# Gate logits with the turned tokens held still and eight gate columns moving, and counts one sub-step after them

## The chip, the cores and the metric

The kernel runs on one core of a Trainium2 chip. The metric is the device time of one execution in microseconds, the median of several runs. The profile is of one execution; its engines are called PE (matmuls; PEld are its weight loads), DVE, ACT, POOL and SP, and SP issues most of the transfers.

## What is computed

A causal long convolution of x (8 x 5696 x 128) with a filter h of the same length, by FFT, and on its output a mixture of eight experts in which each token goes to the one expert with the largest gate logit:

```
y = irfft(rfft(x, 2*S) * rfft(h, 2*S))[:, :S]        # x: (8, 5696, 128), h: (5696, 128)
y = y.reshape(45568, 128)
logits = y @ w_gate                                   # w_gate: (128, 8)
e = argmax(logits); p = softmax(logits)[e]            # one expert a token
out = p * (relu(y @ w1[e]) @ w2[e])                   # w1: (8, 128, 1024), w2: (8, 1024, 128)
```

## The kernel before

The batch is worked in three groups of 2, 3 and 3 sequences. Each group passes three stages: `phase_a` (one half of the forward transform, PSUM tiles `pa`), `phase_b` (the other half, product with the filter's spectrum, first half of the inverse) and `phase_c`, the last half of the inverse with the gating. Tokens are then scattered by POOL, row by row, into a DRAM table `SR` that is sorted by expert, and the experts work on tiles of 256 sorted rows.

`phase_c` goes over slots (16 in the first group, 24 in the second and third) of six blocks of 120 tokens, each slot in two sub-steps of three blocks. One sub-step (the loop over `n` and `k`) issues:
- `synth`: the inverse transform's matmuls into `yp`. `settle` copies them to `rt`, the rows that will be scattered, after the `yield`; the DVE addition at its start (line 739 of before) writes the row numbers once a slot.
- `turn`: three transposes (`flip`, line 182) of `rt` into the PSUM tile `tp`, one sub-step after `synth`. `turned` copies them to `yt`, 128 features by 120 tokens a block.
- `logit`: two sub-steps after `synth`, three matmuls that hold the gate's columns (padded to 32) and move a block of 120 tokens, each into its own 32 rows of the tail of `tp`. Each is two instructions on PE, since the data is plain float32. `logit_out` copies the 96 x 120 strip to `lt` on ACT.
- `score`, in the first sub-step of a slot only: into the PSUM tile `gb` go the counts of the slot before (one-hot `oh` times a matrix of ones and times a triangle), and the two strips of this slot, transposed so that tokens lie on partitions.
- a step or two of the next group's `phase_a` (`guest`), whose matmuls write `pa`.

After the `yield`, DVE runs `route` (`lmax`, `ls`, `w`, `wm`, the one-hot `oh`, the weight of the row) of one slot and `rank` (running counts `cum`, `base`, the row's place `rk`, `pi`) of the slot before it, their instructions alternating (`zipped`). `divide` splits the next input into two parts (`vr`, on ACT and DVE). `rank` puts six scatters on the list `sorts`; `sort_one` issues them on POOL, each tied to one of the PE or ACT instructions of its sub-step. When the last slot of a part of the tokens is ranked, `tables` works out which expert each tile of that part has, and the tile's gathers (`xr`, from `SR`) and weights (`wb`) may be issued on SP.

The experts are one stream, `pipeline`: an expert step is `mh` (line 1147, first layer, two 128-column pieces), ACT and DVE make `hs` of it, and two steps later `ma` (line 1168, second layer). Four steps make a tile; the input rows of a tile are turned in `mx`, printed as `mxNone` for the first. There are 182 tiles, 26 of them of the first part of the tokens; a tile is usable when its part is sorted, tabled and some virtual time old (`SETTLED`).

The order of all this on each engine is not written out. `run` holds a virtual time for each stream, takes the one that is earliest and adds what it yields: an expert step yields `STEP` (1420), a sub-step of `phase_c` yields `STEP` times `BESIDE` or `ENDING`, or less while it is `alone`. Engines then run in the order in which instructions were issued. PSUM tiles of `phase_c` rotate through four banks (`cx`) beside the experts.

## Time and profile before

| | us |
|---|---|
| median of 3 runs (lowest, highest) | 2227.01 (2226.05, 2228.76) |
| the profiled execution | 2223.97 |
| its span in the profile | 2222.2 |
| gating of the first group, alone | about 278 to 400 |
| scatters end, first expert tiles start | about 400 to 445 |
| second group's `phase_b`, then its gating | 445 to 716, 716 to 958 |
| its end, before the third group's `phase_b` | 958 to 1010 |
| third group's gating | 1353 to 1616 |
| expert tiles alone | from about 1680 to the end |

The mean granted TensorE clock was 0.976. Times within the profile count from the start of the span. The bounds of the stages are read from the lines that are active; experts run beside all that comes after about 430. In the rows, `L182` and the like are lines of the kernel before, `out<-in` names the tile written and those read, and an `x6` behind a row is a group of six instructions that follow each other. "Idle before" in brackets is how long the engine had nothing to run, and what ended that.

### The profile page before, as it was taken

What the parts mean: (1) busy time and instruction counts of PE and PEld (TensorE: products, weight loads), DVE (VectorE), ACT (ScalarE), POOL (GpSimd) and SP (SyncE); (2) the same over time, 40 slices, a digit from 0 to 9 for tenths busy, and PEclk for the clock granted to TensorE, in tenths of its full rate; (3) what the DMA queues carried; (4) which work ended last, traced back from release to release, by engine and by line L of the source; (5) the groups of instructions that cost most, each with busy time, mean ns of one, the idle gap of its engine ahead of it and who ended that gap; (6) DMA issues with size and microseconds to landing.
All of it is one profiled execution on the core that took longest, in us unless ns stands there. A gap on an engine that the chain in (4) does not pass through costs nothing. (4 is left out here: it accounts for less than half of the span.)

```text
span 2222.2 us, 47032 instructions
## 1 busy us (share of the span) xinstructions
PE 2078.4 (94%) x14198; PEld 1753.2 (79%) x14198; DVE 1556.4 (70%) x3731; ACT 1100.6 (50%) x2359; POOL 1285.2 (58%) x1486
## 2 busy tenths in 40 slices
PE   7899888599999999988999999999998999999997
PEld 5688655366667888876777779888888999999997
DVE  3588745599997788868988985777764555555554
ACT  4588644233334666643443445555544444444443
POOL 5366548776663388872565661787873444444442
PEclk9999999899999999999999999999999999999999
DMA  9889999699998888967898977777644543444430
GB/s 296 289 280 322 315 348 305 174 277 267 287 283 227 236 272 240 261 195 208 244 263 227 261 242 210 196 204 199 182 152 151 172 139 109 146 138 144 139 121 27
DMA packets 235225, 486.04 MB, mean 219 GB/s; under 512 B 33285, under 2 KB 147074, under 8 KB 234971
## 3 DMA queue, kind: packets, MB, share of 16 engines
q1 hardware_dynamic: 211035, 435.93, 65.4%
q0 software_dynamic: 23936, 47.09, 6.8%
q8 instruction: 115, 1.88, 0.4%
q14 instruction: 139, 1.14, 0.2%
HBM read 593.26 MB, written 173.52 MB: 345 GB/s over the span
## 5 line engine op out<-in xcount | busy, mean ns | idle before, releaser
L1155 DVE SCALAR_TENSOR_TENSOR hs<-mh,hs 128x512 fp32r<-128x512 f32 x728 | 500.8, 690 | 398.3 <-ACT hs L1153 326.9
L1147 PE MATMUL mh<-xtb,wb 128*128 128x256 f32 x4368 | 690.0, 294 | 33.9 <-DMA wb<-WD 18.7
L1153 ACT ACTIVATE hs<-mh 128x512 fp32r<-128x512 f32 x728 | 435.0, 598 | 495.3 <-PE mh L1147 379.5
L1147 PEld LDWEIGHTS mh<-xtb,wb 128*128 128x128 f32 x4368 | 585.6, 190 | 103.3 <-issue 44.8
L1168 PE MATMUL ma<-hs,wb 128*128 128x256 f32 x4368 | 655.8, 286 | 7.8 <-DMA wb<-WD 7.8
L1168 PEld LDWEIGHTS ma<-hs,wb 128*128 128x128 f32 x4368 | 568.3, 190 | 9.4 <-DMA wb<-WD 9.1
L644 POOL DMA_INDIRECT SR<-rt,pi x384 | 401.1, 1045 | 208.7 <-PE pa L305 52.3
L1223 POOL DMA_INDIRECT out<-xr x252 | 245.8, 975 | 311.2 <-DVE xr L1186 267.9
L544 POOL TENSOR_TENSOR zt<-zt,xs 128x384 f32<-128x384 f32 (+1 forms) x280 | 297.3, 1071 | 113.0 <-DVE xs L536 86.7
L568 ACT COPY vt<-vp 96x384 f32<-96x384 f32 (+1 forms) x300 | 148.9, 496 | 344.3 <-PE vp L553 314.6
L553 PE MATMUL vp<-zt,mi 128*96 128x384 f32 (+1 forms) x720 | 258.4, 454 | 8.7 <-DVE xs L536 5.3
L517 PE MATMUL xp<-uq,mt 96*128 96x384 f32 (+1 forms) x720 | 262.2, 460 | 3.1 <-ACT vt L568 1.1
L529 DVE TENSOR_TENSOR zt<-xp,hh 128x384 f32<-128x384 f32 (+1 forms) x300 | 174.0, 580 | 59.9 <-PE xp L517 54.7
L1223 POOL DMA_INDIRECT out<-xb x112 | 109.1, 974 | 169.0 <-ACT ot L1178 109.1
L553 PEld LDWEIGHTS vp<-zt,mi 128*96 128x96 f32 x720 | 112.4, 163 | 102.8 <-issue 53.5
L536 DVE SCALAR_TENSOR_TENSOR xs<-xp,hh 64x384 f32<-64x384 f32 (+1 forms) x300 | 175.7, 586 | 6.0
L305 PE MATMUL pa<-xc,fcr 120*120 120x512 f32 x576 | 165.6, 419 | 14.3 <-ACT xc L283 6.4
L534 DVE TENSOR_TENSOR xs<-xp,hh 64x384 f32<-64x384 f32 (+1 forms) x300 | 173.2, 577 | 6.0
L638 POOL TENSOR_TENSOR c_fcs<-c_fcs 120x64 f32<-120x64 f32 (+2 forms) x384 | 154.7, 403 | 11.4
L517 PEld LDWEIGHTS xp<-uq,mt 96*128 96x128 f32 x720 | 123.8, 195 | 33.9 <-issue 15.5
L305 PEld LDWEIGHTS pa<-xc,fcr 120*120 120x120 f32 x576 | 98.2, 186 | 49.6 <-ACT xc L283 7.2
L319 DVE COPY ut<-pa 120x512 f32<-120x512 f32 x96 | 65.9, 687 | 92.9 <-PE pa L305 81.6
(128 smaller groups left out, 2304.4 us busy)
## 6 DMA issues: line engine op xcount, KB each, us to landing
wb<-WD SPq DMA_DIRECT2D x728, 512.0 KB
vq<-V SPq DMA_DIRECT2D x64, 720.0 KB
U<-ut SPq DMA_DIRECT2D x48, 720.0 KB
uq<-U SPq DMA_DIRECT2D x60, 576.0 KB
V<-vt SPq DMA_DIRECT2D x60, 576.0 KB
xr<-SR SPq DMA_DIRECT2D x182, 130.0 KB
xt<-x SPq DMA_DIRECT2D x96, 240.0 KB
hh<-HS SPq DMA_DIRECT2D x120, 192.0 KB
```

Of the source, the lines that this page charges most:

```text
L305: done = nc.tensor.matmul(banks[m][:QN, :], lhs, rhs, start=(k == 0), stop=(k == len(ops) - 1))
L517: nc.tensor.matmul(xj, mt[:, k0 + j, :], uc.rearrange("p (b d) -> p b d", d=D), start=True, stop=True)
L529: nc.vector.tensor_tensor(out=zt, in0=x3, in1=hv[:, 0].broadcast_to([P] + wide), op=ALU.mult)
L536: nc.vector.scalar_tensor_tensor(out=xs[to], in0=x3[at], scalar=-1.0, in1=him, op0=ALU.mult, op1=ALU.mult)
L544: eng.tensor_tensor(out=zt, in0=zt, in1=xs, op=ALU.add)
L553: nc.tensor.matmul(vp[:K2, j * cw : (j + 1) * cw].rearrange("p (b d) -> p b d", d=D), mi[:, k0 + j, :], zt.rearrange("p b (j d) -> p b j d ...
L644: s = nc.gpsimd.indirect_dma_start(out=SR[:, :], out_offset=IndirectOffsetOnAxis(ap=pi[:, b : b + 1], axis=0), in_=rt[:, b, :], in_offset= ...
L1147: nc.tensor.matmul(hp[:, u, :], wb[:, a, f, :], xt[:, b, :], start=(n == 0), stop=(n == 2))
L1153: done = nc.scalar.activation(hs[:, 0], hp, AF.Relu)
L1155: nc.vector.scalar_tensor_tensor(out=hs[:, 1], in0=hp, scalar=0.0, in1=hs[:, 0].bitcast(F32), op0=ALU.max, op1=ALU.subtract)
L1168: nc.tensor.matmul(accs[t], wb[:, a, f, :], hs[:, b, u, :], start=(k == 0 and u == 0 and n == 0), stop=(k == NPAIR - 1 and u == 1 and n == 2),
L1223: sc = nc.gpsimd.indirect_dma_start(out=out[:, :], out_offset=IndirectOffsetOnAxis(ap=xr[:, s, D + 1 : D + 2].bitcast(I32), axis=0), in_=x ...
```

## The change

The logits are made by matmuls whose stationary operand is the turned block `yt` (128 x 120) and whose moving operand is the gate's eight columns, so that tokens come out on partitions and eight columns a block lie side by side. There are six for a slot, two instructions each, all in one sub-step, three after the `synth` of the slot's first half. `logit`, `logit_out`, the strips `lt` and their transposes are gone, and the tile `gb` holds logits only. The counts of a slot are made in the sub-step after its logits, in the tail of that sub-step's `tp`, behind the guest's `pa` (while the group is alone, in a bank of their own). `rank` follows in that sub-step together with `weigh` (the row's weight, formerly the end of `route`), and `route` stands alone in the other. The ranks of a slot thus come two sub-steps earlier than before, and the loop is two sub-steps shorter. The guest hands back all of its instructions as ties for scatters, the wait in `tables` is one `yield` shorter, and the small constants are 24 columns narrower.

```diff
...
-LOGIT = (2, 2, 2)
...
-    wg = part_of(32)
+    wg = part_of(E)
...
-            done = None
+            done = []
             for _ in range(min(count, self.M - self.m)):
-                done = self.step(self.m)
+                done.append(self.step(self.m))
                 self.open.append(self.m)
                 self.m += 1
             return done
...
-        lgs, cnts, lbank, lts = {}, {}, {}, {}
-
...
-        def score(n, m):
+        lgs, cnts, exps, ranks = {}, {}, {}, {}
+
+        def score(n):
             sp = bank(f"gb{g}_{n}", "mx")
-            if 0 <= m < nu:
-                oh2 = gates[m].rearrange("p b e -> p (b e)")
-                nc.tensor.matmul(sp[:, :w], ones, oh2, start=True, stop=True)
-                nc.tensor.matmul(sp[:MP, 128 : 128 + w], lt, oh2, start=True, stop=True)
-                cnts[m] = (
-                    sp[:, :w].rearrange("p (b e) -> p b e", e=E1),
-                    sp[:MP, 128 : 128 + w].rearrange("p (b e) -> p b e", e=E1),
-                )
-            if 0 <= n < nu:
-                lw = 32 * cb
-                for k in range(nsub):
-                    flip(sp[:MP, 256 + k * lw : 256 + (k + 1) * lw], lts.pop((n, k)), lw)
-                lgs[n] = sp[:MP, 256 : 256 + ns * 32].rearrange("p (b e) -> p b e", e=32)[:, :, :E]
+            lg = sp[:MP, : ns * E].rearrange("p (b e) -> p b e", e=E)
+            yt = yts.pop(n)
+            for b in range(ns):
+                nc.tensor.matmul(lg[:, b], yt[:, b, :], wg, start=True, stop=True)
+            lgs[n] = lg
+
+        def count(n, tp):
+            if state["alone"] or tp is None:
+                cb_, lo = bank(f"cb{g}_{n}", "mx"), 0
+            else:
+                cb_, lo = tp, 512 - 2 * w
+            oh2 = gates[n].rearrange("p b e -> p (b e)")
+            nc.tensor.matmul(cb_[:, lo : lo + w], ones, oh2, start=True, stop=True)
+            nc.tensor.matmul(cb_[:MP, lo + w : lo + 2 * w], lt, oh2, start=True, stop=True)
+            cnts[n] = (
+                cb_[:, lo : lo + w].rearrange("p (b e) -> p b e", e=E1),
+                cb_[:MP, lo + w : lo + 2 * w].rearrange("p (b e) -> p b e", e=E1),
+            )
 
         def route(n):
-            rt = rts[n]
...
             gates[n] = oh
-            yield
+
+        def weigh(n):
+            rt, ex = rts[n], exps.pop(n)
...
             with nc.allow_low_precision("whole numbers"):
                 nc.vector.tensor_reduce(out=pi, in_=rk, axis=AX.X, op=ALU.add)
-            yield
-            for b in range(ns):
-                sorts.append((pi, rt, b, closes.get(n) if b == ns - 1 else None))
+            ranks[n] = pi
...
-        TL, LL = TURN[g], LOGIT[g]
+        TL = TURN[g]
         total_sub = nu * nsub
...
+        read, known_ = nsub + TL, nsub + TL + 1
+
+        def slot_of(at, lag):
+            n, k = divmod(at - lag, nsub)
+            return n if k == 0 and 0 <= n < nu else None
+
+        for at in range(total_sub + TL + 2):
+            n, k = divmod(at, nsub)
+            if parts[0].ready and state["prepped"]:
+                state["alone"] = False
+            if k == 0:
+                load(n + 2)
+            made = turning = tp = None
+            carried = []
+            scored, counted = slot_of(at, read), slot_of(at, known_)
+            if n < nu:
+                made = synth(n, k)
+            if 0 <= at - TL < total_sub:
+                tp = bank(f"tp{g}_{n}_{k}", "mh")
+                turning = turn(*divmod(at - TL, nsub), tp)
+            if scored is not None:
+                score(scored)
+            if guest:
+                few = n < QUIET[g] or scored is not None and not state["alone"] and g
+                carried = guest.begin(1 if few else 2)
+            if counted is not None:
+                count(counted, tp)
+            most = 3 if len(sorts) > 8 else PER_SUB[g]
+            ties = [made, *carried] if len(carried) >= most - 1 else [made, turning, *carried]
+            ties = [x for x in ties if x is not None]
+            for x in ties if len(ties) <= most else ties[:1] + ties[len(ties) - most + 1 :]:
+                sort_one(x)
+            if state["alone"]:
+                yield cost if n < nu else cost / 2
+            else:
+                yield STEP * (BESIDE if n < nu else ENDING)[g]
+            if guest:
+                guest.end()
+                if guest.m >= guest.M and not guest.over and guest.done():
+                    finished[0] = at
+            if finished[0] is not None and at >= finished[0] + 4 and n >= nu - EAGER[g] and ahead[0] < 2:
+                next(after)
+                ahead[0] += 1
+            if n < nu:
+                divide(*divmod(at + AHEAD, nsub))
+                settle(n, k)
+            if 0 <= at - TL < total_sub:
+                turned(*divmod(at - TL, nsub))
+            chains = []
+            if counted is not None:
+                chains += [rank(counted), weigh(counted)]
+            if scored is not None:
+                chains.append(route(scored))
+            zipped(*chains)
+            if counted is not None:
+                rt, pi = rts.pop(counted), ranks.pop(counted)
+                for b in range(ns):
+                    sorts.append((pi, rt, b, closes.get(counted) if b == ns - 1 else None))
+                if counted in closes:
+                    pt = closes[counted]
+                    chores.append(tables(pt, state["base"]))
+                    if pt is parts[-1]:
+                        chores.append(fill(pt, state["base"]))
+            chore(3 if state["alone"] is False else 10)
...
         nc.tensor.matmul(at, unit, ge.rearrange("p c j -> p (c j)"), start=True, stop=True)
-        yield LATER
...
-    place(np.pad(moe_w_gate, ((0, 0), (0, 32 - E))))
+    place(moe_w_gate)
...
```

What the change moves, at three places.

PE in the third group. Names: the first number after a tile's name is its group's slot, the second the half; `mh` and `ma` are experts. Before, a sub-step with counts and strips:

```order
L182 MATMUL tp_11_0_20901<-ident,rt_10_20773 128x120 x3
L770 MATMUL tp_11_0_20901<-yt_10_20888,c_small 32x120 x3
L792 LDWEIGHTS ones
L792 MATMUL gb_9_20908<-oh_8_20797,ones 128x54
L793 LDWEIGHTS c_small
L793 MATMUL gb_9_20908<-oh_8_20797,c_small 120x54
L182 MATMUL gb_9_20908<-ident,lt_9_0_20777 120x96
L182 MATMUL gb_9_20908<-ident,lt_9_1_20890 120x96
L1147 MATMUL mh_1_20925<-xtb_20834,wb_0_17951 128x256 x6
L1168 MATMUL ma_20763<-hs_3_20851,wb_3_4580 128x256 x6
L1147 MATMUL mh_2_20967<-xtb_20834,wb_1_17953 128x256 x6
L182 MATMUL mx_77_20974<-ident,ot_20945 128x128 x2
```

The change, the sub-step with logits and the start of the next one with counts, of the same slot 10:

```order
L181 MATMUL tp_11_1_20839<-ident,rt_11_20810 128x120 x3
L770 MATMUL gb_10_20843<-c_small,yt_10_20717 120x8 x6
L1130 MATMUL mh_1_20862<-xtb_20757,wb_0_4409 128x256 x6
L1151 MATMUL ma_20706<-hs_3_20774,wb_3_17715 128x256 x6
L1130 MATMUL mh_2_20904<-xtb_20757,wb_1_4411 128x256 x6
L181 MATMUL mx_78_20911<-ident,ot_20882 128x128 x2
L181 MATMUL mx_78_20911<-ident,xr_20423 128x128 x2
L1151 MATMUL ma_20916<-hs_0_20854,wb_2_4413 128x256 x6
L729 MATMUL yp_12_0_20943<-vr_12_0_20807,gcr 120x384 x6
L181 MATMUL tp_12_0_20950<-ident,rt_11_20810 128x120 x3
L779 LDWEIGHTS ones
L779 MATMUL tp_12_0_20950<-oh_10_20939,ones 128x54
```

The counts of slot 10 now follow its logits after two `mh`, two `ma`, one `yp` and one turn; before, `gb_9` counted slot 8, whose logits stood in the `gb` of a whole slot earlier.

DVE at the same place. Before, routing of slot 10 and ranking of slot 9 alternate behind `vr` and the row numbers `rt`; `oh_10` is the next row but one:

```order
L718 TENSOR_TENSOR vr_13_0_21222<-vq_13_20892,vr_13_0_21222 120x768
L739 TENSOR_TENSOR rt_12_21225<-c_small 120x6
L847 COPY cum_9_21231<-base_9_20996 128x9
L850 TENSOR_TENSOR cum_9_21231<-gb_10_21124,base_9_20996 128x9
L808 TENSOR_REDUCE lmax_10_21235<-gb_10_21124 120x6
L850 TENSOR_TENSOR cum_9_21231<-gb_10_21124,cum_9_21231 128x9
L812 TENSOR_TENSOR ls_10_21238<-gb_10_21124,lmax_10_21235 120x48
L850 TENSOR_TENSOR cum_9_21231<-gb_10_21124,cum_9_21231 128x9
L822 SCALAR_TENSOR_TENSOR w_120<-ls_10_21238,c_small 120x3x8 x2
L850 TENSOR_TENSOR cum_9_21231<-gb_10_21124,cum_9_21231 128x9
L827 TENSOR_REDUCE wm_10_21246<-w_120 120x6
L850 TENSOR_TENSOR cum_9_21231<-gb_10_21124,cum_9_21231 128x9
```

The change:

```order
L1138 SCALAR_TENSOR_TENSOR hs_0_20854<-mh_0_20794,hs_0_20854 128x512
L1138 SCALAR_TENSOR_TENSOR hs_1_20875<-mh_1_20862,hs_1_20875 128x512
L717 TENSOR_TENSOR vr_12_1_20923<-vq_12_20525,vr_12_1_20923 120x768
L789 TENSOR_REDUCE lmax_10_20929<-gb_10_20843 120x6
L793 TENSOR_TENSOR ls_10_20931<-gb_10_20843,lmax_10_20929 120x48
L803 SCALAR_TENSOR_TENSOR w_120<-ls_10_20931,c_small 120x3x8 x2
L808 TENSOR_REDUCE wm_10_20937<-w_120 120x6
L812 TENSOR_TENSOR oh_10_20939<-w_120,wm_10_20937 120x54
L1138 SCALAR_TENSOR_TENSOR hs_2_20960<-mh_2_20904,hs_2_20960 128x512
```

Routing now follows `vr` directly; `cum` and the row numbers stand in the other sub-step.

PE and SP at the end of the first group. PE before, from the last `gb` to the first expert matmul:

```order
L792 LDWEIGHTS ones
L792 MATMUL gb_14_4508<-oh_13_4434,ones 128x54
L793 LDWEIGHTS c_small
L793 MATMUL gb_14_4508<-oh_13_4434,c_small 120x54
L182 MATMUL gb_14_4508<-ident,lt_14_0_4413 120x96
L182 MATMUL gb_14_4508<-ident,lt_14_1_4499 120x96
L182 MATMUL mxNone_4582<-ident,xr_4530 128x128 x2
L770 MATMUL tp_16_1_4619<-yt_15_4497,c_small 32x120 x3
L1147 MATMUL mh_0_4630<-xtb_4627,wb_0_4574 128x256 x6
```

PE in the change:

```order
L181 MATMUL mxNone_4461<-ident,xr_4426 128x128 x2
L729 MATMUL yp_15_1_4490<-vq_15_4089,c_small 120x384 x2
L181 MATMUL tp_15_1_4493<-ident,rt_15_4468 128x120 x3
L770 MATMUL gb_14_4497<-c_small,yt_14_4353 120x8 x6
L304 MATMUL pa_35_0_4504<-xc_35_4375,fcr 120x512 x3
L304 MATMUL pa_35_1_4508<-xc_35_4375,fcr 120x512 x3
L1130 MATMUL mh_0_4527<-xtb_4524,wb_0_4409 128x256 x6
L181 MATMUL tp_16_0_4554<-ident,rt_15_4468 128x120 x3
```

The first expert input is turned before the last inverse transform of the group, and `yp`, turns, logits and two `pa` stand between it and the first `mh`. SP before, where the first gathers stand ahead of the first weights:

```order
L1098 DMA xr_4552<-SR 128x260
L1096 TENSOR_LOAD tab_4446
L1096 ISA x2
L1098 ISA
L1098 DMA xr_4563<-SR 128x260
L1109 TENSOR_LOAD tab_4446
L1109 ISA x2
L1118 ISA
L1118 DMA wb_0_4574<-WD 128x1024
L1118 ISA
L1118 DMA wb_1_4576<-WD 128x1024
```

SP in the change:

```order
L1101 DMA wb_0_4409<-WD 128x1024
L1101 ISA
L1101 DMA wb_1_4411<-WD 128x1024
L1101 ISA
L1101 DMA wb_2_4413<-WD 128x1024
L1101 ISA
L1101 DMA wb_3_4415<-WD 128x1024
L1079 TENSOR_LOAD tab_4238
L1079 ISA x2
L1081 ISA
L1081 DMA xr_4426<-SR 128x260
```

The weights of the first tile now stand ahead of the first gather.

PE in the second group, slots 12 and 13. Before:

```order
L730 MATMUL yp_12_1_10680<-vr_12_1_10527,gcr 120x384 x6
L182 MATMUL tp_12_1_10687<-ident,rt_12_10644 128x120 x3
L770 MATMUL tp_12_1_10687<-yt_11_10531,c_small 32x120 x3
L305 MATMUL pa_19_1_10694<-xc_19_10483,fcr 120x512 x3
L305 MATMUL pa_20_0_10703<-xc_20_10575,fcr 120x512 x3
L1147 MATMUL mh_3_10726<-xtb_10390,wb_1_4576 128x256 x6
L1168 MATMUL ma_10631<-hs_1_10590,wb_2_4578 128x256 x6
L730 MATMUL yp_13_0_10751<-vr_13_0_10641,gcr 120x384 x6
L182 MATMUL tp_13_0_10758<-ident,rt_12_10644 128x120 x3
L770 MATMUL tp_13_0_10758<-yt_12_10745,c_small 32x120 x3
```

The change:

```order
L729 MATMUL yp_12_1_10691<-vr_12_1_10602,gcr 120x384 x6
L181 MATMUL tp_12_1_10698<-ident,rt_12_10669 128x120 x3
L770 MATMUL gb_11_10702<-c_small,yt_11_10606 120x8 x6
L304 MATMUL pa_19_1_10709<-xc_19_10578,fcr 120x512 x3
L729 MATMUL yp_13_0_10788<-vr_13_0_10666,gcr 120x384 x6
L181 MATMUL tp_13_0_10795<-ident,rt_12_10669 128x120 x3
L304 MATMUL pa_20_0_10804<-xc_20_10639,fcr 120x512 x3
L304 MATMUL pa_20_1_10808<-xc_20_10639,fcr 120x512 x3
L779 LDWEIGHTS ones
L779 MATMUL tp_13_0_10795<-oh_11_10784,ones 128x54
L780 LDWEIGHTS c_small
L780 MATMUL tp_13_0_10795<-oh_11_10784,c_small 120x54
```

Before, each sub-step has an `mh` and an `ma`; in the change five sub-steps around slots 11 to 13 have none, since the next tile is not usable yet by the virtual time.

More of the change, by code (lines that the diff above doesn't have):

```diff
@@ L762, in turned @@
             nc.scalar.copy(yts[n][:, k * cb : (k + 1) * cb, :], tv)
-        lgs, cnts, lbank, lts = {}, {}, {}, {}
-        def logit(n, k, tp):
-            yt = yts[n]
-            lp = tp[:, 512 - MP :]
-            for b in range(cb):
-                done = nc.tensor.matmul(
-                    lp[32 * b : 32 * b + 32, :MP],
-                    wg,
-                    yt[:, k * cb + b, :],
-                    start=True,
-                    stop=True,
-                    tile_position=(0, 32 * b),
-                )
-            lbank[n, k] = lp
-            if k == nsub - 1:
-                yts.pop(n)
-            return done.ins
@@ L813, in route @@
             yield
-            ex = sb.tile([MP, ns, E], F32, tag="ex", name=f"ex{g}_{n}")
-            nc.scalar.activation(ex, ls, AF.Exp)
+            exps[n] = sb.tile([MP, ns, E], F32, tag="ex", name=f"ex{g}_{n}")
+            nc.scalar.activation(exps[n], ls, AF.Exp)
             w9 = state["w9"][n % 2][:, :ns]
@@ L887, in phase_c @@
         finished, ahead = [None], [0]
-        TL, LL = TURN[g], LOGIT[g]
+        TL = TURN[g]
         total_sub = nu * nsub
-        sl = (LL + nsub - 1) // nsub + 1
-        n_end = nu + sl + 1
-        for n in range(n_end + 1):
-            for k in range(nsub):
-                at = n * nsub + k
-                if parts[0].ready and state["prepped"]:
-                    state["alone"] = False
-                if k == 0:
-                    load(n + 2)
-                made = turning = read = carried = None
-                if n < nu:
-                    made = synth(n, k)
-                if TL <= at < total_sub + LL:
-                    tp = bank(f"tp{g}_{n}_{k}", "mh")
-                if 0 <= at - TL < total_sub:
-                    turning = turn(*divmod(at - TL, nsub), tp)
-                if 0 <= at - LL < total_sub:
-                    read = logit(*divmod(at - LL, nsub), tp)
-                if k == 0 and n >= sl:
-                    score(n - sl, n - sl - 1)
-                if guest:
-                    few = n < QUIET[g] or k == 0 and n >= sl and not state["alone"] and g
-                    carried = guest.begin(1 if few else 2)
-                ties = [made, read, carried] if carried else [made, turning, read]
-                ties = [x for x in ties if x is not None]
-                count = 3 if len(sorts) > 8 else PER_SUB[g]
-                for x in ties if len(ties) <= count else ties[:1] + ties[len(ties) - count + 1 :]:
-                    sort_one(x)
-                if state["alone"]:
-                    yield cost if n < nu else cost / 2
-                else:
-                    yield STEP * (BESIDE if n < nu else ENDING)[g]
-                if guest:
-                    guest.end()
-                    if guest.m >= guest.M and not guest.over and guest.done():
-                        finished[0] = at
-                if finished[0] is not None and at >= finished[0] + 4 and n >= nu - EAGER[g] and ahead[0] < 2:
-                    next(after)
-                    ahead[0] += 1
-                if n < nu:
-                    divide(*divmod(at + AHEAD, nsub))
-                    settle(n, k)
-                if 0 <= at - TL < total_sub:
-                    turned(*divmod(at - TL, nsub))
-                if 0 <= at - LL < total_sub:
-                    logit_out(*divmod(at - LL, nsub))
-                if k == 0:
-                    chains = []
-                    if 0 <= n - sl - 1 < nu:
-                        chains.append(rank(n - sl - 1))
-                    if 0 <= n - sl < nu:
-                        chains.append(route(n - sl))
-                    zipped(*chains)
-                    if n - sl - 1 in closes:
-                        pt = closes[n - sl - 1]
-                        chores.append(tables(pt, state["base"]))
-                        if pt is parts[-1]:
-                            chores.append(fill(pt, state["base"]))
-                chore(3 if state["alone"] is False else 10)
-                if at >= total_sub + LL:
-                    break
```

9 lines of the change are left out of this document (2 added, 7 removed).

## Prediction

> **What bounds the kernel now.** I read the page's busy line first, then a table of stretches cut at the stage borders, then groups of instructions by form, then the timeline of one slot. The page:
>
> ```profile
> PE 2078.4 (94%) x14198; PEld 1753.2 (79%) x14198; DVE 1556.4 (70%) x3731; ACT 1100.6 (50%) x2359; POOL 1285.2 (58%) x1486
> ```
>
> TensorE is busy 94% of the span, so a change in its work counts where it is really full. The stretches below are the first group's gating stage, the second group's, the end of that one, and the third group's (columns: length; busy time of PE, PEld, DVE, ACT, POOL; granted clock; DMA share; GB/s):
>
> ```profile
> 278.00:400.00 122.00, 108.99 (x571) 64.75 (x572) 64.00 (x300) 58.61 (x150) 83.60 (x124) 0.98 0.91 310
> 716.00:958.00 242.00, 234.76 (x1723) 202.22 (x1723) 191.30 (x651) 156.41 (x362) 173.18 (x229) 0.99 0.85 250
> 958.00:1010.00 52.00, 39.42 (x270) 35.04 (x269) 32.47 (x127) 15.83 (x36) 34.19 (x53) 0.87 0.71 195
> 1353.00:1616.00 263.00, 255.92 (x2119) 233.77 (x2118) 184.84 (x619) 153.49 (x362) 182.09 (x239) 1.00 0.70 197
> ```
>
> In the second and third groups' gating PE is busy 97% (234.76 of 242; 255.92 of 263): 48 of the 64 slots, where a microsecond of TensorE is a microsecond of the span. In the first group's (16 slots) it is 89%, DMA 91%, and the end is set by the scatters, shown below; there I take PE's saving or cost as nothing.
>
> **Matmuls removed.** Two sub-steps of the third group on PE (start, duration of the group, operation; overlapping durations, so I use starts):
>
> ```profile
> 1533.15 0.47 PE L182 MATMUL tp<-ident,rt 120*128 120x120 f32 x3
> 1533.55 0.41 PE L770 MATMUL tp<-yt,c_small 128*32 128x120 f32 x6
> 1533.88 0.20 PE L792 MATMUL gb<-oh,ones 120*128 120x54 bf16 x1
> 1533.98 0.36 PE L182 MATMUL gb<-ident,lt 96*120 96x96 f32 x2
> 1534.12 0.94 PE L1147 MATMUL mh<-xtb,wb 128*128 128x256 f32 x6
> 1534.90 0.87 PE L1168 MATMUL ma<-hs,wb 128*128 128x256 f32 x6
> 1535.61 0.86 PE L1147 MATMUL mh<-xtb,wb 128*128 128x256 f32 x6
> 1536.30 0.87 PE L1168 MATMUL ma<-hs,wb 128*128 128x256 f32 x6
> 1537.01 1.22 PE L730 MATMUL yp<-vr,gcr 120*120 120x384 f32 x6
> 1538.06 0.47 PE L182 MATMUL tp<-ident,rt 120*128 120x120 f32 x3
> 1538.80 0.97 PE L1147 MATMUL mh<-xtb,wb 128*128 128x256 f32 x6
> 1539.61 0.88 PE L1168 MATMUL ma<-hs,wb 128*128 128x256 f32 x6
> ```
>
> From the first turn to the first `ma`: 1533.15 to 1534.90 is 1.75 us in the sub-step with counts, 1538.06 to 1539.61 is 1.55 in the other. Without gating there would be three turns at about 0.10 (an estimate from the 0.40 between 1533.15 and 1533.55, which has a gap in it) and an `mh` of 0.69 (1535.61 to 1536.30): 1.00. So column logits, strip turns and counts cost 0.75 + 0.55 = 1.30 us a slot.
>
> **Matmuls added.** Per slot twelve loads of a 128x120 tile (two passes of six blocks) and twelve matmuls of eight columns, and the two counts at another place. No row shows an 8-column float matmul, but one with few columns cannot hide a load of 120, so I price the loads. Their rows (mean ns of one is the number behind the comma):
>
> ```profile
> L770 PEld LDWEIGHTS tp<-yt,c_small 128*32 128x32 f32 x768 | 19.4, 108 | 21.4 <-issue 16.6 <-ACT yt L762 1.8 <-ACT hs L1153 1.1
> L730 PEld LDWEIGHTS yp<-vq,c_small 120*120 120x120 f32 x128 | 22.4, 191 | 42.6 <-issue 16.6 <-ACT rt L746 12.2 <-ACT ut L319 4.8
> L182 PEld LDWEIGHTS tp<-ident,rt 120*128 120x128 f32 x384 | 49.0, 141 | 14.8 <-issue 6.2 <-ACT rt L746 1.0
> L1147 PEld LDWEIGHTS mh<-xtb,wb 128*128 128x128 f32 x4368 | 585.6, 190 | 103.3 <-issue 44.8 <-DVE hs L1155 18.6 <-ACT hs L1153 3.4
> ```
> ```profile
> 905.55 0.18 PEld L305 LDWEIGHTS pa<-xc,fcr 120*120 120x120 f32 x1
> 905.65 0.18 PEld L305 LDWEIGHTS pa<-xc,fcr 120*120 120x120 f32 x1
> ```
>
> A load lasts 0.18 to 0.19 us, but the two `pa` loads start 0.10 apart. The slope from 32 to 128 columns is (190 − 108)/96 = 0.85 ns a column, 102 ns for 120: the same. The transposing load is cheaper: (141 − 108)/96 = 0.34, or with the same 81 ns of fixed latency taken off, (141 − 81)/128 = 0.47 ns a column, 56 ns for 120. Those turns are of plain float data like `yt`, but they run in one pass, with the identity moving; the logits run in two passes. I take 0.105 as the nearest (a full load beside a full load): 12 × 0.105 = 1.26, and 0.15 for counts that stand alone (L792 to the strip turns, 1533.88 to 1533.98, is 0.10). Sum 1.41 against 1.30: +0.11 a slot, × 48 = **+5 us**. Ends: 0.056 gives 0.67 + 0.15 = 0.82, −0.48 a slot, −23 us; a whole 0.19 gives +1.1 a slot, +54 us, which the two `pa` loads exclude for loads that follow each other.
>
> [...]
>
> **Work taken off ACT and DVE.** The strip copies (two a slot on ACT) and the wide strided logits go. ACT is busy 153.49 of 263 in the third group: nothing for the end. DVE loses nothing in kind, but its order changes, which is the next term.
>
> **Counts one sub-step after the logits.** In the kernel before, a slot's one-hot `oh` is made in one score sub-step and counted two sub-steps later. Now the logits come in one sub-step and the counts in the next, so `oh` must be ready when PE is through `mh`, `ma`, `mh`, `ma`, `yp` and the turns. By the rows above this is from the end of the gating, 1534.2, to 1538.37 (1538.06 + 3 × 0.10): about 4.2 us. DVE's work there:
>
> ```profile
> 1536.52 0.96 DVE L718 TENSOR_TENSOR vr<-vq,vr 120x768 fp32r<-120x768 f32 x1
> 1537.39 0.35 DVE L739 TENSOR_TENSOR rt<-c_small 120x6 int32<-120x6 f32 x1
> 1537.81 0.20 DVE L808 TENSOR_REDUCE lmax<-gb 120x6 f32<-120x48 f32 x1
> 1539.05 0.38 DVE L831 TENSOR_TENSOR oh<-w,wm 120x54 bf16<-120x54 f32 x1
> ```
> ```profile
> 294.45 0.21 DVE L808 TENSOR_REDUCE lmax<-gb 120x6 f32<-120x48 f32 x1 [0.82 <-PE gb L182]
> 295.56 0.22 DVE L831 TENSOR_TENSOR oh<-w,wm 120x54 bf16<-120x54 f32 x1
> ```
>
> `vr` stands ahead of the routing in both orders and ends at about 1537.4. In the new order L739 and the count additions fall in the other sub-step, so the routing runs as in the first slot, where nothing is interleaved: 294.45 to 295.78, 1.33 us. `oh` would end at 1537.4 + 1.35 = 1538.8, 0.43 us after PE asks for it, in each of 24 slots: **+10 us**. Behind the waiting count on PE stand the next `mh` and `ma`, so nothing fills it. Ends: 0 (if `vr` also comes earlier, since ACT has fewer copies) and twice that, +20 (if the delay of `mh` comes back as a later `hs` and `vr`). In the second group two `pa` of about 0.8 us each stand between the turns and the count, which is cover enough for the same chain; without them it would be the same 0.4 a slot.
>
> **End of the first group.** Scatters on POOL, the gathers `xr` and weights `wb` on SP, and the first expert work on PE:
>
> ```profile
> 292.00 1.45 PE L730 MATMUL yp<-vq,c_small 120*120 120x384 f32 x4
> 299.10 1.13 PE L730 MATMUL yp<-vq,c_small 120*120 120x384 f32 x3
> 306.96 1.15 POOL L644 DMA_INDIRECT SR<-rt,pi  x1 [5.18 <-DVE xc L284]
> 417.38 1.01 POOL L644 DMA_INDIRECT SR<-rt,pi  x1 [0.19 <-DVE ls L812]
> 424.32 3.92 SPq L1098 DMA_DIRECT2D xr<-SR  x4
> 426.69 0.69 PE L182 MATMUL mxNone<-ident,xr 128*128 128x128 f32 x2 [9.93 <-DMA xr<-SR]
> 433.51 1.62 PE L1147 MATMUL mh<-xtb,wb 128*128 128x256 f32 x6 [5.58 <-DMA wb<-WD]
> ```
>
> 72 scatters from 306.96 to 417.38 are 1.56 us each, so the end follows from when they may begin. Ranks come two sub-steps earlier, 7.1 us by the two `yp` rows: `xr` at 417.2, X at 419.6. The order also puts the first `wb` ahead of `xr` on SP, and a `yp`, turns, logits and two `pa` (about 4.5 us) between X and the first `mh`: about 425 against 433.5, less 1.5 us of gating that is left over after it: **−7 us**. Ends: 0 (scatters bound by data, not by ranks) and −13 (433.51 to 420.5, no work between).
>
> **Second group.** The experts start earlier and stand eight steps further on in the new order when this stage begins; they run out of ready tiles, and five sub-steps (slots 11 to 13) carry no expert step. A sub-step is 242/48 = 5.0 us, of which an expert step is 1.4; what is left keeps PE less full. I take 0.6 us of idle each: **+3 us** (0 to +9). At the stage's end three waits stand in the way of PE:
>
> ```profile
> 968.49 0.41 PE L770 MATMUL tp<-yt,c_small 128*32 128x120 f32 x6 [1.40 <-ACT yt L762]
> 971.79 0.97 PE L1147 MATMUL mh<-xtb,wb 128*128 128x256 f32 x6 [1.26 <-DVE pi L861]
> 981.90 0.18 PE L792 MATMUL gb<-oh,ones 120*128 120x54 bf16 x1 [2.28 <-DVE oh L831]
> ```
>
> The last count and ranks come two sub-steps earlier: 4.9 us of waits, of which I take **−2**. The final stage after the third group has the same tiles, and I leave it.
>
> **Sum.** −7 + 5 + 3 − 2 + 10 = +9. The profiled execution took 2223.97 (span 2222.2 and 1.8 around it); the median is 3.0 above it. Added to the median, 2227.0 + 9 = **2236 us**.
>
> **Rivals.**
> A, faster: the loads go at the transposing rate of 56 ns, or hide behind the short matmuls. For it: those turns, too, load plain float data. Against it: every full load in the rows is at 0.10 or more. Then −23 instead of +5: 2236 − 28 = 2208. It decides from about 0.08 us a load.
> B, no change: `oh` comes in time in the third group, because ACT's missing copies let `vr` come 0.4 us earlier. The sum without +10 is −1: 2226. Against it: `vr` begins right behind `hs`, whose place follows `mh`, not ACT's load.
> C, slower still: the wait in the third group feeds itself and is 0.85 a slot (+20), and the first group's end does not move because scatters are set by their data: −7 goes to about −3. 2236 + 10 + 4 = 2250.
> [...]
>
> **Chances.** Forecast 0.50 (its own range 2229 to 2245), A 0.15, B 0.20, C 0.13, D 0.02. Range 2203 to 2251: from A with a little more gain at the first group's end, to C; D and the far ends are left out. A measurement of this kernel tells about 0.2%, 4.5 us, from no change. Faster (under 2222.5): A's 0.15 and 0.07 of B, 0.22. Same: 0.13 of B and 0.06 of the forecast's low end, 0.19. Slower: 0.59.
>
> **What would show it.** Loads: PE from the first turn to the first `ma` in the third group's logit sub-steps, now 1.55, should be about 2.25 to 2.4, and 1.25 in the others; at 1.7, A holds. Waits: the count's row in 1353 to 1616 should carry an idle of 0.4 put down to DVE `oh`. First group: the first `mh` after the scatters near 425 instead of 433.5. Second group: PE idle in the sub-steps of slots 11 to 13. The prediction is wrong if a load costs under 0.08 us, or if the routing starts before `vr`.

## The result, and the profile after

The change is slower: 2254.8 us median (2250.6 to 2260.1, four runs) against 2226.5 us for the kernel before beside it, ratio 1.0132 (95% interval 1.0103 to 1.0162), about +28 us. Measured a second time it was 1.0151 (1.0124 to 1.0179). The sign was forecast; +9 us was not enough, and 2254.8 lies above the range. The profiled execution took 2255.89, span 2254.1.

The busy line of the page after:

```profile
PE 2105.7 (93%) x14070; PEld 1816.5 (81%) x14070; DVE 1586.1 (70%) x3731; ACT 1076.9 (48%) x2231; POOL 1282.9 (57%) x1486
```

PE is 27 us busier although it has 128 matmuls fewer, and ACT has lost the 128 strip copies. To find the place I cut both traces at the same program points: the first and last `yp` of each group, the end of the first group's last `pa`, the first `xp` of the next `phase_b`, the end of its last `vp`. Lengths in us, with how many expert steps had begun at the first point in brackets; "before" is the range over four profiles of that kernel (before, before_b, before_c, before_d), "after" gives two of the change (after, after_b):

| stretch | before | after |
|---|---|---|
| first group: first `yp` to last `pa` | 134.7 to 141.0 [0] | 152.4, 147.9 [0] |
| from there to the first `xp` | 25.5 to 29.3 [0] | 31.8, 30.4 [0.2] |
| second group's `phase_b` | 256.5 to 257.1 [5] | 255.7, 255.7 [13] |
| its last `vp` to the first `yp` | 14.3 to 14.6 [61] | 24.3, 25.3 [69] |
| second group's gating | 238.7 to 242.9 [69] | 241.0, 240.6 [77] |
| its last `yp` to the next `xp` | 33.7 to 41.1 [125] | 44.3, 43.7 [128] |
| third group's `phase_b` | 331.9 to 335.7 [139] | 336.3, 336.7 [141] |
| its last `vp` to the first `yp` | 20.1 to 21.4 [244] | 23.3, 23.8 [246] |
| third group's gating | 262.2 to 263.5 [257] | 268.2, 266.7 [259] |
| its last `yp` to the last expert step | 584.3 to 590.1 [360] | 582.1, 583.0 [362] |

Windows of the kernel before, then of the changed one, for the places that differ (columns as in the prediction): the first group from its eighth sub-step, the stretch ahead of the second group's gating, and the end of that group.

```profile
307.49:415.73 108.24, 95.00 (x508) 56.36 (x509) 63.95 (x324) 50.91 (x133) 92.92 (x140) 0.98 0.83 271
701.25:715.80 14.55, 12.42 (x105) 12.01 (x104) 6.79 (x13) 7.16 (x15) 2.16 (x3) 1.00 0.79 218
957.89:997.27 39.38, 30.07 (x228) 27.19 (x227) 23.64 (x103) 13.79 (x32) 31.07 (x48) 0.91 0.66 184
```
```profile
306.68:428.91 122.23, 105.82 (x485) 71.26 (x486) 70.89 (x326) 47.05 (x109) 97.72 (x149) 0.92 0.84 276
716.45:740.79 24.34, 14.00 (x104) 13.00 (x104) 10.40 (x17) 9.38 (x18) 2.16 (x3) 0.90 0.88 248
740.79:981.83 241.04, 234.78 (x1612) 213.04 (x1611) 194.30 (x655) 144.34 (x308) 180.82 (x244) 0.97 0.81 236
981.83:1026.15 44.32, 29.52 (x213) 27.28 (x211) 20.10 (x81) 11.19 (x25) 26.04 (x40) 0.84 0.72 195
1385.77:1654.02 268.25, 259.48 (x2064) 253.66 (x2065) 200.47 (x637) 146.09 (x317) 191.06 (x249) 0.99 0.69 190
```

In the first group PE is 10.8 us busier at a mean granted clock of 0.92 in place of 0.98. Ahead of the second group's gating the same 7.7 expert steps take 24.3 us in place of 14.6, with the same PE work. The PE timeline there shows why:

```profile
723.80 0.95 PE L1130 MATMUL mh<-xtb,wb 128*128 128x256 f32 x6 [2.01 <-DMA wb<-WD]
739.34 1.65 PE L1151 MATMUL ma<-hs,wb 128*128 128x256 f32 x6 [6.97 <-DMA wb<-WD]
740.79 1.48 PE L729 MATMUL yp<-vr,gcr 120*120 120x384 f32 x4
```

The expert step stands in front of the group's first `yp` on PE and waits 6.97 us for weights. The logits themselves, in the third group's slot, cost what was forecast (the group of loads, then PE):

```profile
1564.66 1.34 PEld L770 LDWEIGHTS gb<-c_small,yt 128*120 128x120 f32 x12
```
```profile
1564.45 0.47 PE L181 MATMUL tp<-ident,rt 120*128 120x120 f32 x3
1564.76 1.33 PE L770 MATMUL gb<-c_small,yt 128*120 128x8 f32 x12
1565.94 0.96 PE L1130 MATMUL mh<-xtb,wb 128*128 128x256 f32 x6
1566.74 0.88 PE L1151 MATMUL ma<-hs,wb 128*128 128x256 f32 x6
1569.94 0.47 PE L181 MATMUL tp<-ident,rt 120*128 120x120 f32 x3
1570.76 0.18 PE L779 MATMUL tp<-oh,ones 120*128 120x54 bf16 x1 [0.35 <-DVE oh L812]
```

Twelve loads start over 1.34 − 0.185 = 1.155 us, 0.105 each; from the first turn to the first `ma` it is 2.29 us (forecast 2.25 to 2.4). And the count waits 0.35 us for `oh` (forecast 0.4).

### The profile page after: what moved, and what is told of

It reads as the page before. It is cut to its first block, busy times and chain, and to the rows that moved or that the text cites. A ratio compares the mean times of both kernels' runs of the same rounds, so it can differ in the third digit from the quotient of the medians.

```text
span 2254.1 us, 46643 instructions
## 1 busy us (share of the span) xinstructions
PE 2105.7 (93%) x14070; PEld 1816.5 (81%) x14070; DVE 1586.1 (70%) x3731; ACT 1076.9 (48%) x2231; POOL 1282.9 (57%) x1486
## 5 line engine op out<-in xcount | busy, mean ns | idle before, releaser
L1130 PE MATMUL mh<-xtb,wb 128*128 128x256 f32 x4368 | 698.8, 296 | 29.3 <-DMA wb<-WD 24.2
L1151 PEld LDWEIGHTS ma<-hs,wb 128*128 128x128 f32 x4368 | 574.1, 191 | 18.7 <-DMA wb<-WD 18.4
L643 POOL DMA_INDIRECT SR<-rt,pi x384 | 409.5, 1066 | 224.3 <-issue 55.1
L1206 POOL DMA_INDIRECT out<-xr x262 | 255.6, 976 | 347.9 <-DVE xr L1169 294.3
L1206 POOL DMA_INDIRECT out<-xb x102 | 99.5, 976 | 147.8 <-ACT ot L1161 102.6
L637 POOL TENSOR_TENSOR c_fcs<-c_fcs 120x64 f32<-120x64 f32 (+2 forms) x384 | 143.3, 373 | 11.3
```

The costliest lines, as they stand in the source:

```text
L643: s = nc.gpsimd.indirect_dma_start(out=SR[:, :], out_offset=IndirectOffsetOnAxis(ap=pi[:, b : b + 1], axis=0), in_=rt[:, b, :], in_offset= ...
L1130: nc.tensor.matmul(hp[:, u, :], wb[:, a, f, :], xt[:, b, :], start=(n == 0), stop=(n == 2))
L1151: nc.tensor.matmul(accs[t], wb[:, a, f, :], hs[:, b, u, :], start=(k == 0 and u == 0 and n == 0), stop=(k == NPAIR - 1 and u == 1 and n == 2),
L1206: sc = nc.gpsimd.indirect_dma_start(out=out[:, :], out_offset=IndirectOffsetOnAxis(ap=xr[:, s, D + 1 : D + 2].bitcast(I32), axis=0), in_=x ...
```

## The experiments

Ratios are to the kernel before on the same chip, with 95% intervals.

**form_only.** The kernel before with the new logits at the place of the strip transposes.

```diff
-                    flip(sp[:MP, 256 + k * lw : 256 + (k + 1) * lw], lts.pop((n, k)), lw)
+                for b in range(ns):
+                    nc.tensor.matmul(lg[:, b], yt[:, b, :], wg[:, :E], start=True, stop=True)
```

> The kernel before with one part of the change alone: the logits of a slot are six matmuls with the turned tile held still and eight gate columns moving, made where the strips were transposed before; counts, ranks, scatters and all expert steps stand where they stood. Theory (the time went into the moved schedule): the twelve loads cost 1.26 us against 1.2 us of strips, so about +0.1 us a slot and 2227 to 2234 us, the second group starting with the same expert step as before. Rival (the form itself costs the time, on TensorE or by the clock): 2245 us or more.

1.0151 (1.0122 to 1.0180), 2238.9 us: the rival's side, though for a reason that neither named. The first group is 134.8 long, as before; the second group's gating is 249.6 and the third's 273.0, 7 to 11 us more each, where the +0.11 us a slot of the prediction makes 2.6. The waits in front of PE, from groups of instructions in the second group's gating and in the third's:

```profile
L305 PE MATMUL pa<-xc,fcr 120*120 120x512 f32 x216 | 66.5, 421 | 11.5 <-DVE rk L834 10.7 <-ACT ut L319 0.7
```
```profile
L1122 PE MATMUL mh<-xtb,wb 128*128 128x256 f32 x621 | 97.5, 292 | 10.3 <-DVE hs L1130 8.9 <-ACT hs L1128 1.5
```

The kernel before has 2.8 to 3.4 for `rk` and 2.9 to 3.7 for `hs` there. My reading is that all of PE's gating now lies in one sub-step, and the other is too short to cover the chain of ranks and routing on VectorE. late_all, next, has the counts one sub-step later: there `rk` is down to 0.3, `hs` to nothing, and the ratio to 1.0074 on the same chip. So moving the counts, as the change does, is what the new form needs. The two stages hold 17 to 22 us of form_only's 31; the rest was not placed.

**late_all, late_g0, hold_g0.** The change with its ranks back in their old place, in all groups or in the first; and the change with early ranks, but the first group's scatters held back.

```diff
-        read, known_ = nsub + TL, nsub + TL + 1
+        read = nsub + TL + 2      # late_g0: 2 in the first group, else 0
+        known_ = read + 1
...
-                    sorts.append((pi, rt, b, ...))
+                    kept.append((at + 3, (pi, rt, b, ...)))   # hold_g0, first group
```

> The change with logits and counts two sub-steps later in all groups: ranks and expert steps stand where they did before, the counts still follow their logits by one sub-step. Theory: as late_g0, 2230 to 2240 us, with the wait for the one-hot of about 0.25 us a slot left in the third group. Rival (the ranks' place in the second and third groups matters): more than 5 us away from late_g0.

> The change with logits and counts of the first group two sub-steps later (ranks where they were before), the other groups as in the change. Theory (early ranks of the first group start its scatters 10 us earlier into a stretch where DMA is full, PE stalls and loses its clock; and the experts' lead of eight steps puts a weight load into the stretch before the second group's gating): the first group's gating takes within 4 us of before's, the stretch ahead of the second group's gating loses its 10 us, and the whole is 2230 to 2240 us. Rival (the first group loses its 13 us to the form or to the single PSUM bank that logits and counts share there): that stage stays 10 us or more longer than before, 2243 us or more.

> The change with its early ranks, but the first group's scatters are put on the list three sub-steps later, so that they start where they did before. Theory (scatters against the full DMA): the first group's gating takes within 4 us of before's and the first expert work is no earlier than before; 2237 to 2247 us, since four or five steps of lead are left. Rival (bank or form): that stage stays 10 us or more longer, 2250 us or more.

Ratios 1.0074 (1.0048 to 1.0100), 1.0118 (1.0068 to 1.0168) and 1.0110 (1.0081 to 1.0138); medians 2225.0, 2228.2, 2230.9 us on a chip on which the kernel before took 2207.7, so that the figures in us of the expectations do not compare and the stages must. The first group takes 134.1, 134.5 and 135.8 us in the three, against 152.4 and 147.9 in the change and 134.7 to 141.0 in the kernel before: what the theory said of the stage. In shares of 2226.5 us the whole was expected at 1.002 to 1.006 (late_all, late_g0) and 1.005 to 1.009 (hold_g0), and all three are above it. The stretch ahead of the second group's gating is 14.5 and 14.7 without the lead, 20.6 in hold_g0, which keeps five steps of it. The form and the shared PSUM bank are the same in hold_g0 as in the change, so they alone are not what lengthens the first group; the early start of the scatters is, with what hangs on it (the first `mxNone`, too, is back behind the group's last `yp`). Over all profiles but twice, the stage takes 144.4 to 152.4 us in the three with early scatters (after, after_b, no_lead) and 133.7 to 141.9 in the thirteen without. For the whole kernel this is less plain: the intervals of late_g0 and hold_g0 overlap that of the change, 1.0103 to 1.0162. The window of hold_g0 answers to that of the change above, clock 1.00 against 0.92:

```profile
308.07:414.46 106.39, 97.12 (x484) 65.71 (x485) 69.57 (x325) 46.90 (x108) 91.13 (x140) 1.00 0.88 291
```

**before_b, after_b, no_lead.** Both kernels once more on one chip, and the change with the experts' start put off.

```diff
-SETTLED = (2840, 8000, 8000)
+SETTLED = (11840, 8000, 8000)
```

> The kernel before, unchanged, for a profile on the same chip as the runs beside it: the stages of 445 to 1616 us should have the lengths of the first profile within 2 us (257, 242, 336, 263 us), if the chips differ in the stages that DMA bounds; if they differ everywhere, every stage is shorter by about 1%.

> The change, unchanged, for a profile on the same chip. A ratio of 1.010 to 1.016 again. Theory (early scatters stall the first group): its gating again takes 8 us or more longer than in the kernel before beside it. Rival (the stall in the first profile was that run's own): within 4 us, and the loss stands elsewhere.

> The change, with the experts' start put off (the first number of SETTLED 2840 to 11840), so that the second group's gating starts with expert tile 17 in its step 2 and not tile 19 in step 1 (before: tile 17, step 1). Early ranks and early scatters stay. Theory (the lead costs more than it brings: a weight load in the stretch ahead of the second group's gating, five sub-steps without an expert step, a load at the end of the second group): the 7 us weight wait ahead of that stage goes, no sub-step is without an expert step, ratio 1.003 to 1.009. Rival (those waits do not hang on the lead): ratio 1.013 or more, since the earlier start is given up.

before_b agrees with the first profile within 2 us in every stage named, but its whole span is only 1.6 us shorter, so it does not tell in which stages the chips differ. after_b repeats the change's loss and its places; the first group up to its last `pa` is 7 us longer than in before_b (15 in the first pair), of which only 2.6 lie before the last `yp`: under the 8 us of the theory, above the 4 of its rival. The size of the stall varies. no_lead is 1.0065 (1.0045 to 1.0084), so giving up seven steps of head start makes the kernel 0.9%, or 21 us, faster, with early ranks and early scatters kept. In the profiles, 12.4 us of the gain on after_b lie ahead of the second group's gating, 7.3 ahead of its `phase_b`, 9.9 in the third group's `phase_b` and the stretch behind it; the end of the second group and the last stretch take 7.6 us more. The stretch ahead of the second group's gating and that gating in no_lead:

```profile
704.61:717.51 12.90, 12.30 (x104) 12.09 (x104) 7.18 (x13) 7.48 (x15) 1.96 (x2) 1.00 0.80 212
717.51:956.91 239.40, 235.81 (x1676) 215.43 (x1675) 200.33 (x669) 148.96 (x319) 180.30 (x243) 1.00 0.86 254
```

12.9 us in place of 24.3, and 56 expert steps in 239.4 us where the change has 51 in 241.0.

**late_count_later, route_first.** late_all with one edit each, in the third group: the counts one more sub-step later; the routing issued ahead of the split of the next input.

```diff
+        known_ = read + (2 if g == 2 else 1)       # late_count_later
...
+            if scored is not None and g == 2:      # route_first
+                zipped(route(scored))
             if n < nu:
                 divide(*divmod(at + AHEAD, nsub))
```

> As late_all (logits and counts two sub-steps later), and in the third group the counts two sub-steps after their logits in place of one. Theory: the wait of TensorE for the one-hot there (7 us in late_all) goes, ratio 1.003 to 1.005. Rival (the wait only moves, to the vector chain or to hs): 1.006 to 1.009 as late_all's 1.007.

> late_all with one edit: in the third group the routing is issued ahead of the split of the next input (vr), so the one-hot does not stand behind 1 us of vr on VectorE. Theory (the place of vr on VectorE sets when the one-hot comes): the 7 us of waits of the count for the one-hot fall under 1 us, the third group's gating is 3 us or more shorter than in late_all. Rival (the wait moves to hs or to vr, as when the counts came later): the stage stays within 2 us of late_all's or grows.

late_count_later: 1.0122 (1.0096 to 1.0148), the rival, and worse than it said: the third group's gating is 272.5 us in place of 265.0 to 265.5. route_first: 1.0035 (1.0020 to 1.0051), the theory: 259.5 us. PE's waits in that stage in late_all_b, in late_count_later, and the count in route_first:

```profile
L779 PE MATMUL tp<-oh,ones 120*128 120x54 bf16 x21 | 3.9, 185 | 7.2 <-DVE oh L812 4.9 <-issue 1.4 <-DVE wm L808 0.5
```
```profile
L1132 PE MATMUL mh<-xtb,wb 128*128 128x256 f32 x618 | 97.1, 292 | 13.8 <-DVE hs L1140 8.8 <-ACT vr L716 3.3 <-ACT hs L1138 1.6
```
```profile
L779 PE MATMUL tp<-oh,ones 120*128 120x54 bf16 x21 | 4.0, 188 | 0.0
```

With the count later, routing and ranking meet again in one sub-step on VectorE, and `mh` waits for `hs` behind them. With `vr` behind the routing, the wait is gone, and nothing takes its place: the stage is then 2.7 to 4.0 us shorter than in the kernel before.

**late_all_b, twice.** late_all again beside a profile of the kernel before (before_c), and late_all with the twelve logit matmuls issued twice.

```diff
+            for _ in range(2):
                 for b in range(ns):
                     nc.tensor.matmul(lg[:, b], yt[:, b, :], wg, start=True, stop=True)
```

> The kernel before, unchanged, for a profile beside the next three on the same chip.

> late_all once more (logits and counts two sub-steps later, all experts' steps where they stood before), beside a profile of the kernel before: ratio 1.002 to 1.010. Theory (dearer logits and the wait for the one-hot): the second group's gating within 2 us of before's, the third group's 3 to 8 us longer, the other stages alike. Rival (the loss stands where DMA sets the time): the stages of 278 to 445 or 958 to 1010 us carry it.

> late_all with the twelve logit matmuls of each slot, loads and all, issued twice over the same place. Theory (TensorE is the bound of both stages, a load costs 0.105 us there): 12 x 0.105 = 1.26 us a slot more, in the second group 25 to 30 us, in the third 18 to 30 us (the longer gating covers the wait for the one-hot), 40 to 60 us in all on late_all. Rival (other engines set these stages, or loads hide): under 25 us.

late_all_b: 1.0069 (1.0043 to 1.0096); 11.1 us longer in its span than before_c, spread over the stages (first group +1.4, `phase_b` +3.1 and +2.4, third gating +2.7, end +2.3; second gating −3.3). So neither the theory's list nor the rival's holds the loss. twice: 1.0546 (1.0509 to 1.0584), far above the 40 to 60 us expected: against late_all_b the first group is 35.5 us longer, the second gating 34.8, the third 40.0, so 1.45 and 1.67 us a slot in the last two, not 1.26. The granted clock is lower, too, which is enough for the rest but was not tried apart. In the last two stages it is 0.94 and 0.93, where late_all_b has 0.99 and 1.00:

```profile
753.20:1027.60 274.40, 272.12 (x1913) 252.81 (x1914) 200.11 (x650) 151.16 (x318) 176.81 (x237) 0.94 0.76 221
1422.00:1727.00 305.00, 299.49 (x2306) 294.85 (x2307) 195.38 (x616) 146.55 (x317) 181.07 (x240) 0.93 0.63 170
```

**first_as_before, first_changed, before_d.** The change (as in route_first) in the second and third groups only; the change (as in late_all) in the first only. Both also have the wait in `tables` and the width of the small constants as in the kernel before.

```diff
-            yield from phase_c(gr, guests[gr.g], after)
+            yield from (phase_c if gr.g else phase_c0)(gr, guests[gr.g], after)   # phase_c0: the loop before
```

> The first group's gating as in the kernel before (its logits, strips, counts and places), the second and third groups as in route_first (logits with the turned tile held still, counts one sub-step later, routing ahead of vr in the third). Theory (what is left of the loss in late_all and route_first stands in the first group, where the load-heavy logits and waits lower the granted clock): ratio 0.996 to 1.000, with the second and third gating 5 us shorter together. Rival (the loss hangs on the second and third groups or their scatters): 1.003 or more as route_first.

> The complement: the first group's gating as in late_all (changed logits, counts one sub-step after them, ranks where they stood before), the second and third groups as in the kernel before. Theory: 1.002 to 1.006, the loss of route_first without its gains. Rival: 0.999 to 1.001.

> The kernel before, unchanged, for a profile on the same chip as these two.

first_as_before is **0.9967** (0.9950 to 0.9983), 2200.9 against 2206.7 us: a little faster than the kernel before, and so than the change. first_changed is 1.0018 (1.0002 to 1.0033), between the rival's range and the theory's, with an interval that reaches into both; its first group takes 133.7 us, no more than before_d's 134.7, so the profile does not put its loss there. In the profiles the third group's gating takes 258.3 us against 262.3 in before_d, but the second's 240.5 against 238.7: the 5 us expected of both together are 2, and the stretch after the last `yp` gives another 6 (578.2 against 584.3), which no run here explains.

```profile
1345.20:1603.50 258.30, 254.31 (x2054) 247.54 (x2055) 198.44 (x617) 146.65 (x317) 181.56 (x237) 1.00 0.71 200
```
```profile
1337.40:1599.70 262.30, 255.64 (x2117) 233.83 (x2118) 184.62 (x620) 152.99 (x361) 182.97 (x238) 1.00 0.69 196
```

## Why the prediction was wrong, step by step

Two steps failed. The −7 booked an earlier start of the experts as time saved; it made later stages longer, and putting that start off saves 21 us. And the first group's gating, put at nothing, became 7 to 18 us longer. The terms in the order of the sum:

**Loads, +5: right in the price, too small in the sum.** 0.105 us a load was measured: in the logits at 1564.66 full-height loads of 0.185 us and matmuls of 0.25 us (medians over the 768 of each in the change) follow each other every 0.105, so a load and its matmul do not run one behind the other, which would be 0.435 a pair. Rival A falls, since it decided from about 0.08. From the first turn to the first `ma` of the third group, sub-steps without `mx` take 2.29 us (median) with logits and, where nothing waits (route_first), 1.24 with counts, against 1.55 and 1.75 before: +0.23 a slot in place of +0.11, or +11 in 48 slots by the same sum. My own signs, 2.25 to 2.4 and 1.25, already summed to 0.20 to 0.35 above the 3.30 of before, and I did not set them against the +0.11.

**Counts behind the logits, +10: right in mechanism, too large.** The wait for `oh` is 5.9 us in 17 waits, 0.35 each, and route_first shows `vr` as its cause. So rival B is out, and C, whose 2250 came nearest, was near by luck: its wait was to be 0.85. But the third group's gating grew by 3 to 6 us only, loads included, where 12.5 were forecast. I added the new wait to the old span and did not look at what it displaces: PE's waits for `hs`, 2.9 to 3.7 us in the four profiles of the kernel before, are gone. `mh` in the third group's gating of before_c and of the change:

```profile
L1147 PE MATMUL mh<-xtb,wb 128*128 128x256 f32 x618 | 96.1, 291 | 5.9 <-DVE hs L1155 3.2 <-ACT hs L1153 0.9 <-DMA wb<-WD 0.9
```
```profile
L1130 PE MATMUL mh<-xtb,wb 128*128 128x256 f32 x618 | 95.2, 290 | 0.6 <-DMA wb<-WD 0.6
```

**End of the first group, −7: half of it came, and it was counted wrongly.** The first `mh` came at 428.7 instead of 433.5 (forecast 425), 427.7 instead of 431.7 in the second pair, and at the first `xp` of `phase_b` the experts are eight steps ahead, worth 8 × 1.4 = 11 us of PE. I booked this as time saved. It was a lead that had to last to the end, and it did not: the stretch ahead of the second group's gating gave back 10 us (the weight wait), that gating five of the steps or 7 us, the end of the group one more; two were left for the last stretch. The forecast had the eight steps and the five empty sub-steps in its own order rows, priced the empty sub-steps at +3, and never asked which expert tile would meet the stretch in which experts run alone. no_lead shows the size: 1.0151 to 1.0065, all that hangs on the experts' start taken together.

**"There I take PE's saving or cost as nothing": the other step that failed.** The first group became 7 to 18 us longer. I treated early scatters as pure gain. They start at 297.4 instead of 307.0 (20.9 us behind the group's first `yp` instead of 28.7), into a stretch in which DMA is at 0.95 to 0.99 of its time (in windows of 10 us from 290 to 360), and DVE waits for a store of `ut`. Here is DVE of the change, where the store is named, then ACT at a second place, where the profile names no releaser and the same wait is likely, then PE, then the clock after it:

```profile
311.46 0.69 DVE L318 COPY ut<-pa 120x512 f32<-120x512 f32 x1 [2.26 <-DMA U<-ut]
```
```profile
354.88 0.58 ACT L318 COPY ut<-pa 120x512 f32<-120x512 f32 x1 [5.80 <-remote]
```
```profile
355.90 1.89 PE L729 MATMUL yp<-vq,c_small 120*120 120x384 f32 x4 [2.70 <-ACT rt L745]
```
```profile
357.00:358.00 1.00, 1.00 (x5) 0.59 (x4) 0.58 (x1) 0.00 (x0) 0.93 (x2) 0.50 0.98 367
358.00:359.00 1.00, 1.00 (x4) 0.82 (x4) 0.00 (x0) 0.00 (x0) 0.37 (x1) 0.50 0.84 286
359.00:360.00 1.00, 1.00 (x4) 0.74 (x3) 0.00 (x0) 0.29 (x1) 0.90 (x2) 0.50 0.87 304
```

PE waits 2.7 us behind ACT, and a microsecond later its clock is 0.50 for more than 3 us. From the eighth sub-step to the last `pa`, the time lost in such drops, half of their length at a clock of 0.50, is 10.4 us in this profile (four drops), 6.0 in after_b and 6.8 in no_lead (two each), and nothing in hold_g0, where the scatters start as before. Of the thirteen profiles without early scatters (twice aside), eight have no such drop and five lose 1.7 to 4.1 us. Two of the change's four drops, at 316 and 384, follow only about 1 us of waits and begin 0.9 and 2.4 us behind a burst of twelve logit matmuls, so the new form may have a share in them; that was not tried. A second cause is in the order I had quoted: `mxNone` stands ahead of the group's last `yp`, and waits for its gather in front of it. From that `yp` to the end of the last `pa` it is 9.4 us (8.9 in after_b) in place of 4.6.

```profile
419.08 0.69 PE L181 MATMUL mxNone<-ident,xr 128*128 128x128 f32 x2 [3.15 <-DMA xr<-SR]
419.56 2.76 PE L729 MATMUL yp<-vq,c_small 120*120 120x384 f32 x4
```

**End of the second group, −2: wrong sign.** It is 44 us with 13 expert steps in place of 34 to 41 with 14, with 11.3 us of waits for weights in front of PE (10.2 in after_b, at most 5.3 in the kernel before). The lead is not needed for it: no_lead has 46 us and 9.3 of such waits. The cause stays open.

What stays open: late_all and late_all_b lose 0.7% without lead and without early scatters, spread over many stages. no_lead, with early scatters and a first group of 144.4 us, loses no more than they do (1.0065, on another chip), so what the longer first group costs the whole kernel is not shown. How much of the 0.7% the first group carries was not settled either: first_changed says 0.2%, route_first against first_as_before 0.7%, but on different chips and with the wait in `tables` changed as well, which no run tries alone. And the first group's own length varies by 6 us between profiles of the kernel before, and by 8 (133.7 to 141.9) over the kernels with late scatters.

## What to carry to other kernels

A head start for a stream is not time saved until one has followed it to the stage that ends the program: see which of its loads and waits then meet which stage. Work that comes earlier was not free here, where it met a full resource (DMA at 0.95 to 0.99 in the change): the first group took 144.4 to 152.4 us with early scatters and 133.7 to 141.9 without (twice aside). And an edit that moves work between two halves of a loop must be judged by what each half still covers: form_only lost 1.5%, and late_count_later 0.5% on late_all, for almost no more work.

## What the runs showed of the hardware

In twice, the granted clock falls behind bursts of matmuls that move eight columns behind full loads, while PE is not idle. Here are a burst of 24 and the windows after it:

```profile
1594.65 2.59 PE L771 MATMUL gb<-c_small,yt 128*120 128x8 f32 x24
1597.09 0.96 PE L1133 MATMUL mh<-xtb,wb 128*128 128x256 f32 x6
1597.89 1.34 PE L1154 MATMUL ma<-hs,wb 128*128 128x256 f32 x6
```
```profile
1597.00:1598.00 1.00, 1.00 (x10) 1.00 (x10) 0.00 (x0) 0.00 (x0) 0.96 (x2) 1.00 0.84 121
1598.00:1599.00 1.00, 1.00 (x7) 1.00 (x6) 0.22 (x1) 0.85 (x2) 0.81 (x2) 0.53 0.68 194
...
1601.00:1602.00 1.00, 1.00 (x7) 1.00 (x7) 0.90 (x5) 0.89 (x3) 0.97 (x2) 0.76 0.24 68
```

PE is busy throughout, and yet the clock is 0.50 from about 1598.07 to 1601.48 (0.53 and 0.76 in the windows that hold its ends), 3.4 us. The second and third groups' gating of twice has 48 such bursts and 21 such drops; all but the first drop begin between 0.7 us before and 1.2 us behind the end of a burst, 19 of them with no idle of PE in the 3.4 us before. Not every burst has a drop. In late_all_b, with twelve such matmuls in a burst, these stages have one drop, just behind the second group's first `yp` (clock 0.99 and 1.00). That the burst brings it on is read from twice against late_all_b; which property of the burst does it was not tried.
